# A new opening order with other fillers, branch hints, and a last store in two parts, in a fused three-layer kernel on one core

## The chip, the core and the metric

The kernel runs on one NeuronCore of a Trainium2 chip. The metric is device time in microseconds. Before the change three runs gave 753.0, 754.3 and 757.43 us, with a median of 754.3. The engines are called PE (TensorE; PEld is its weight load), DVE (VectorE), ACT (ScalarE), POOL (GpSimd) and SP (SyncE, which issues most transfers). A q behind a name (ACTq) marks an engine's sequencer, which runs branches, register loads, semaphore waits and transfer issues.

## The reference

Three layers follow one another on 4 batches of 768 rows and 384 columns, all in float32:

```python
# layer 1, gated linear attention, 4 batches x 8 heads x 768 rows x 48
f = 1.0 / (1.0 + np.exp(-f_logit))
for t in range(S):
    state = f[:, :, t, :, None] * state + einsum('bhd,bhe->bhde', k[:, :, t], v[:, :, t])
    y[:, :, t] = einsum('bhd,bhde->bhe', q[:, :, t], state)
# layer 2, x is y with the heads side by side
xn = (x - mean(x)) / sqrt(var(x) + 1e-06) * g_ln
x = x + maximum(xn @ w_ch1, 0) @ w_ch2             # 384 -> 1536 -> 384
# layer 3
h = maximum(x.T @ w_tok1, 0) @ w_tok2              # over the rows, 768 -> 256 -> 768
u = x + h.T
out = u + maximum(u @ w_ch1b, 0) @ w_ch2b          # 384 -> 1536 -> 384
```

## The kernel before

Layer 1 is cut into chunks of 128 rows: unit n is chunk n // 4 of batch n % 4, 24 units in all. The steps of a unit bear short names, and the prediction uses them. `n.lf`, `n.lq`, `n.lv` load the gate, q and k, and v. `log` and `cum` (L332) build running sums of the log gates with a matmul on a triangle of ones; `ek` and `eq` (L336, L340) take their exponentials on ACT; `km` and `qm` (L343, L346) scale k and q. `kp` (L355) transposes k on PE and `kt` (L246, L248) copies it out. `sc` (L378) forms the scores, `st` (L390) the new state, `A0` and `A1` (L400) mask the scores on DVE. `y` (L441) multiplies masked scores and v; `yw` (L456) is a small ACT operation, named `done` in the rows, that stands between `y` and `z`; `z` (L432) adds what the carried state contributes, in the same PSUM bank (tile `sc`). `stm`, `ste`, `std` carry the state on. `lna`, `lnc`, `lnv` are the layer norm, `tp`, `ah`, `al` the transposes into the MLP. `mS.*` are the pieces of an MLP group of layer 2, the first of its matmuls at L580 and L610.

The MLP weights arrive as 64-bit words and are turned into high and low float32r parts on chip; `wI.ld` is such a load and `wI.a`, `b`, `c`, `h`, `l` are the conversion steps. The big products are made of three matmuls of such parts (hh, lh, hl).

Each piece of work is a slot. Slots are emitted one after another and an engine executes its instructions in the order in which they were emitted, so the emitted order is the schedule of every engine at once, and the order of the transfers on SP too. For the opening, up to the end of unit 11's work, the order is the list `ORDER`, written out step by step; sets beside it choose the engine of a step (`POOL`, `OTHER`) or its PSUM bank (`AT`). Later slots are placed by a planner and stand as before.

A step written `n.step+k` gets fillers on PE ahead of it: matmuls on a tile of zeros that compute nothing. Ahead of `cum`, `kp`, `sc` and `tp` they are k matmuls of 224 columns (`busy`, L536 to L538) into the bank that the step is about to fill. Ahead of `y` they are 3k matmuls of 64 columns (L449) into a part of the `sc` tile. The first work of PE is `warm` (L734), 28 fillers of 224 columns.

The end: the last output chunk is added up on DVE (`fin`, L991), and its store is issued on ACT's queue (`put`, L995), while all earlier stores go through SP. Then each engine loads a flag (L1187) and branches on it (L1194): a general path for inputs outside the fast path's range lies behind that branch and is not taken here. The block after it (L1388) holds the waits for the transfers and the final barrier.

Of the kernel before, what the change touches and what calls it, by code (L numbers as in the profile page):

```python
# [51 lines left out]
ORDER = """
    0.lf 0.log 0.cum 1.lf 1.log 0.lq 0.ek 0.eq 1.cum+4 2.lf 0.lv 0.km 2.log 0.kp+4 0.qm 0.kt 1.eq 3.lf 1.ek 0.tot
    0.sc 1.lq w3.ld 1.tot 0.st 3.log 0.A1 0.A0 2.cum 0.stm 3.cum+9 1.qm 3.ek 0.y 3.tot 0.yw 1.km w3.a 0.z 2.ek
    2.eq 0.lna 1.sc+3 1.lv 2.lq w3.b 4.lf 1.kp w3.c 1.kt w5.ld 5.lf 1.st 0.ste 3.lq 0.lnc 1.A1 1.A0 2.km 1.stm
    0.tp+3 2.tot 3.eq 2.kp 1.y+3 4.log 2.qm 3.qm w5.a 0.lnv 1.yw 1.z 2.sc 0.ah 2.kt 4.cum 5.log 1.lna w5.b 0.al
    3.km 3.kp 2.lv 3.lv w3.h 4.lq 1.lnc 1.ste 2.st w5.c 2.A0 2.A1 1.tp 3.sc w3.l 0.std 4.ek w5.h 5.cum 1.ah w0.ld
    2.stm 2.y 4.eq 3.kt 5.eq 3.st 1.al 4.km 2.ste 3.A0 2.yw 2.z 4.qm 3.A1 3.y w0.a 6.lf 5.ek 4.kp 2.lna 7.lf 3.yw
    6.log 3.stm 2.lnc 4.lv w0.b 3.z w5.l 4.sc 7.log 5.tot 2.tp 4.kt w0.c 4.st w1.ld 6.cum w0.h 7.cum 3.ste 2.ah
    w1.a 3.lna 1.std 4.stm 4.A0 7.tot 4.A1 4.y 7.eq 6.tot 2.al 4.yw w1.b w4.ld 1.lnv 4.tot 5.lq w2.ld w1.c 5.qm  # L60
    m0.5 5.km w1.h w0.l 4.z w2.a 3.lnc 4.ste w16.ld m0.0 w1.l 5.lv 6.eq 6.ek 5.kp 7.ek 5.kt w4.a 5.sc 2.lnv 3.tp
    5.st w16.a w2.b w16.b w2.c m0.h0 w4.b m0.1 6.lq 5.A1 5.A0 m0.h5 3.ah w14.ld 5.stm m0.l5 m0.l0 w16.c 6.qm 4.lna
    5.y m0.3 6.km w13.ld 5.yw 5.z 4.lnc 3.al m0.h1 w2.h 3.lnv 6.kp 6.kt w2.l 5.lna 6.lv w17.ld w4.c 6.sc m0.2
    m0.l1 w14.a 4.tp w15.ld w16.h w14.b w4.h 5.lnc w4.l m0.h3 m0.l3 4.ah w14.c 4.al 6.st 5.tp 5.ah m0.4 m0.h4
    m0.h2 5.al w13.a w14.h 7.lq 7.km 6.A0 w13.b m1.5 w16.l 8.lv 9.lf m0.l2 w12.ld m1.2 m1.3 w12.a 6.A1 2.std m0.l4
    3.std m1.h2 m1.l2 w12.b 6.y 7.qm m1.h3 2.lnr w14.l w12.c 9.log w12.h m1.1 w15.a w7.ld 7.lv m1.h1 w13.c w12.l
    m1.4 5.ste w13.h m1.l3 m1.l1 6.yw 7.sc m1.h4 w15.b w13.l 7.kp w19.ld w11.ld w17.a m1.h5 7.kt w17.b w15.c w15.h
    4.std m1.0 w17.c w15.l m1.h0 m1.l4 m0.o20 7.st w17.h 6.stm m0.o10 w10.ld 8.lf m1.l0 w17.l 7.A0 w7.a m1.l5
    8.log w7.b w11.a w11.b 9.scan 6.z w10.a 9.tot 8.scan w7.c 8.eq 9.lv 6.ste w11.c 8.tot w7.h 7.A1 m1.o10 m0.o00
    8.ek w11.h m1.o11 8.lq m0.o11 m0.o01 8.qm w7.l 4.lnv 8.km w10.b 6.lna 7.y m0.r11 w8.ld 5.lnv m0.o21 m1.7 w19.a  # L70
    5.lnr m0.r01 w9.ld w10.c m0.r21 m1.r11 m1.o00 9.eq w10.h w19.b w10.l w11.l w6.ld w6.a m1.o20 w19.c 6.lnc w6.b
    w9.a 8.kp w9.b m1.o21 9.ek w6.c w19.h w19.l w8.a w8.b w6.h w9.c w20.ld m1.r21 s0.ld w22.ld 8.sc 7.yw 10.lf
    8.kt m1.o01 m1.r01 8.st m1.11 m1.h7 m1.h11 w9.h 8.A1 w6.l w22.a w22.b w8.c 7.stm 11.lf 7.ste w18.ld w21.ld
    10.log m1.6 m0.11 m0.h11 7.z w8.h m1.l11 m1.l7 w9.l m0.6 6.std 9.lq w18.a w18.b w8.l w20.a 9.km m1.h6 w18.c
    m0.7 8.A0 w18.h w20.b w23.ld m0.l11 m0.h6 11.log m0.9 w22.c w18.l w20.c m0.h7 m0.l7 m1.l6 7.lna w20.h m0.l6
    m0.h9 w21.a m1.8 m0.8 w21.b m0.l9 8.y 9.qm w20.l 9.kp 8.stm 7.lnc 10.scan w23.a m1.9 m0.h8 9.kt 8.yw m1.h8
    m1.l8 w23.b 10.ek m1.h9 w21.c m1.10 9.sc m0.l8 m1.h10 8.z w23.c 10.lq s1.ld 10.lv 9.st 8.lna s2.ld m1.l9 5.std
    w23.h 10.eq m0.10 w21.h w23.l 11.scan w21.l m0.o22 m0.h10 w22.h m0.l10 8.ste m1.o02 m1.l10 10.qm 9.A1 7.tp
    7.ah w22.l 6.tp m1.o03 7.lnv 9.A0 7.al 9.y 8.lnc 8.tp m1.r03 m0.o23 11.ek 6.lnv 11.eq 10.tot 10.km s0.a 7.std
    9.yw m1.o12 s1.a 8.lnv 6.ah 9.stm 8.std m0.r23 m1.d0 m0.d2 9.z s0.b 10.sc 10.kp 6.al 8.ah 8.al m0.o02 9.lna  # L80
    10.kt 9.ste m0.o12 9.std s0.c m1.o22 m0.o13 10.st 9.lnc 10.stm s1.b 11.lq m0.r13 m0.o03 s1.c 10.A1 m0.r03
    m1.o13 10.A0 10.ste m1.r13 m0.d1 m0.d0 m1.o23 10.std s3.ld 11.lv m1.d1 8.lnr s0.h
""".split()
# [23 lines left out]
class Slots:
# [1293 lines left out]
```

## Time and profile before

| | us |
|---|---|
| median of three runs | 754.3 (753.0 to 757.43) |
| the profiled execution: its own time | 753.65 |
| its span, first to last instruction | 751.9 |
| PE busy | 741.3 (99% of the span) |
| DVE, ACT, POOL busy | 502.4, 353.7, 119.6 |
| mean granted clock of PE | 0.996 of full speed |

The time of a run holds 1.75 us beyond the span (753.65 - 751.9). PE is busy nearly throughout. From 40 us to 740 us it hardly waits; what it does not use lies in the first 36 us and in the last 6 us.

### The profile page before, as it was taken

How to read it: one execution, taken by the hardware profiler on the slowest of the kernel's cores; microseconds unless marked ns; L12 is line 12 of the kernel's file. 1: busy time of each engine (PE TensorE's matmuls, PEld its weight loads, DVE VectorE, ACT ScalarE, POOL GpSimd, SP SyncE). 2: the span in 40 equal slices, each digit the busy share in tenths (PEclk: the TensorE clock that was granted, in tenths of full speed). 3: DMA queues.
4: the chain of work that ended last, by engine and by line, in shares of the span. 5: the costliest groups of instructions: out<-in, count | busy, mean ns of one | idle time of the engine just before them, and what ended most of it. 6: DMA issues, size and time to landing. Idle time of an engine off the chain costs nothing.

```text
span 751.9 us, 17197 instructions
## 1 busy us (share of the span) xinstructions
PE 741.3 (99%) x6981; PEld 723.5 (96%) x6981; DVE 502.4 (67%) x927; ACT 353.7 (47%) x890; POOL 119.6 (16%) x102
## 2 busy tenths in 40 slices
PE   8999999999999999999999999999999999999996
PEld 7889999999999999999999999999999999999996
DVE  3799886797787767674345655867468654868481
ACT  6756253544645446342223433745266442757340
POOL 2451212122244220200000100101000000102010
PEclk9999999999999999999999999999999999999999
DMA  9775422656576665743438748453433535344401
GB/s 254 225 258 163 148 96 91 216 181 211 160 264 195 186 188 158 218 150 117 128 101 291 268 168 308 144 169 134 135 90 105 176 106 152 95 146 119 119 16 69
DMA packets 62424, 122.52 MB, mean 163 GB/s; under 512 B 7040, under 2 KB 27904, under 8 KB 62336
## 3 DMA queue, kind: packets, MB, share of 16 engines
q1 hardware_dynamic: 62192, 121.14, 51.2%
q8 instruction: 57, 0.93, 0.5%
q14 instruction: 31, 0.25, 0.1%
q10 hardware_dynamic: 144, 0.20, 0.1%
HBM read 96.93 MB, written 24.38 MB: 161 GB/s over the span
## 4 chain that ended last, share of the span: by engine, by line
PE 93%; DVE 3%; ACT 2%; DMA 2%; issue 1%; SPq 0%; ACTq 0%
PE mo L610 20%; PE mo L987 19%; PE mm L580 18%; PE mm L934 18%; PE rt L854 3%; PE ht L876 3%; PE sc L441 2%; DMA cs<-in_w 2%; PE sc L432 2%; PE sc L378 1%; PE sc L390 1%; PE kp L355 1%; PE tp L544 1%; PE tp L888 1%; PE cum L332 1%; PE warm L734 1%
## 5 line engine op out<-in xcount | busy, mean ns | idle before, releaser
L580 PE MATMUL mm<-wx 128*128 128x384 f32 x864 | 159.1, 337 | 0.4 <-DVE hl L599 0.2
L580 PEld LDWEIGHTS mm<-wx 128*128 128x128 f32 x864 | 149.1, 188 | 1.3 <-DVE hl L599 0.8
L934 PE MATMUL mm<-xsh,wx 128*128 128x384 f32 x528 | 138.4, 335 | 0.3 <-DVE q L944 0.3
L610 PE MATMUL mo<-w2h,hh 128*128 128x384 f32 x288 | 98.7, 343 | 0.0
L987 PE MATMUL mo<-w2h,hh 128*128 128x384 f32 x288 | 97.2, 338 | 0.0
L934 PEld LDWEIGHTS mm<-xsh,wx 128*128 128x128 f32 x528 | 95.7, 188 | 1.2 <-DVE q L944 1.2
L610 PE MATMUL mo<-w2h,hl 128*128 128x384 f32 x288 | 96.4, 335 | 0.0
L610 PE MATMUL mo<-w2l,hh 128*128 128x384 f32 x288 | 96.3, 335 | 0.0
L987 PE MATMUL mo<-w2l,hh 128*128 128x384 f32 x288 | 96.3, 334 | 0.0
L987 PE MATMUL mo<-w2h,hl 128*128 128x384 f32 x288 | 96.3, 334 | 0.0
L934 PE MATMUL mm<-xsl,wx 128*128 128x384 f32 x264 | 88.3, 335 | 0.0
L974 POOL TENSOR_TENSOR hl<-u,hh 128x768 fp32r<-128x768 f32 x16 | 29.8, 1861 | 337.0 <-ACT u L969 244.3
L595 ACT ACTIVATE hh<-mm 128x384 fp32r<-128x384 f32 x96 | 46.2, 487 | 74.7 <-PE mm L580 71.3
L599 DVE SCALAR_TENSOR_TENSOR hl<-mm,hh 128x384 fp32r<-128x384 f32 x96 | 52.3, 551 | 20.5 <-ACT hh L595 20.0
L991 DVE TENSOR_TENSOR xr<-mo,xr 128x384 f32<-128x384 f32 x48 | 26.7, 555 | 53.2 <-PE mo L987 53.2
L1150 ACT ACTIVATE cs<-cs 128x384 f32<-128x384 f32 x56 | 31.1, 556 | 57.8 <-DVE cs L1147 57.6
L610 PEld LDWEIGHTS mo<-w2h,hh 128*128 128x128 f32 x288 | 54.1, 188 | 0.3
L987 PEld LDWEIGHTS mo<-w2h,hh 128*128 128x128 f32 x288 | 54.1, 188 | 0.1
L610 PEld LDWEIGHTS mo<-w2l,hh 128*128 128x128 f32 x288 | 54.2, 188 | 0.0
L987 PEld LDWEIGHTS mo<-w2l,hh 128*128 128x128 f32 x288 | 54.1, 188 | 0.0
L987 PEld LDWEIGHTS mo<-w2h,hl 128*128 128x128 f32 x288 | 54.1, 188 | 0.0
L610 PEld LDWEIGHTS mo<-w2h,hl 128*128 128x128 f32 x288 | 54.1, 188 | 0.0
(172 smaller groups left out, 1300.5 us busy)
## 6 DMA issues: line engine op xcount, KB each, us to landing
cs<-in_w SPq DMA_DIRECT2D x48, 384.0 KB, 3.2
sg<-in_w SPq DMA_DIRECT2D x44, 384.0 KB, 4.7
ts<-t_d SPq DMA_DIRECT2D x48, 256.0 KB, 2.9
wx<-f_d SPq DMA_DIRECT2D x12, 576.0 KB, 6.0
V<-in_v_n SPq DMA_DIRECT2D x21, 288.0 KB, 4.8
T<-in_k_t SPq DMA_DIRECT2D x21, 224.0 KB, 2.9
T<-in_q_t SPq DMA_DIRECT2D x21, 224.0 KB, 3.8
x_d<-x SPq DMA_DIRECT2D x24, 192.0 KB, 3.1
```

The source lines that it names most:

```text
L432: nc.tensor.matmul(t["sc"][half(i), r, D * p:D * p + D], t["Q"][rows(r), p, half(i)], s[rows(r), D * p:D * p + D], start=False, stop=p == ...
L580: nc.tensor.matmul(ps, w[:, f, k, :], x[:, k, :], start=(i == 0), stop=(i == 8))
L595: nc.scalar.activation(out=hid(f)[0], in_=t[f], func=AF.Relu)
L599: nc.vector.scalar_tensor_tensor(hl, t[f], 0.0, hh.bitcast(F32), op0=ALU.max, op1=ALU.subtract)
L610: nc.tensor.matmul(ps, x, w[:, f, :], start=(f == lo and i == 0), stop=(f == hi and i == 2))
L854: nc.tensor.matmul(t["r"][j], w, x, start=(s == 0 and i == 0), stop=(s == NCH - 1 and i == 2))
L876: nc.tensor.matmul(ps, w, x[:, j], start=(i == 0), stop=(i == 5))
L934: nc.tensor.matmul(ps, w, x, start=n == 0, stop=n == len(ops) - 1)
L974: le.tensor_tensor(l, whole(g, i), h.bitcast(F32), op=ALU.subtract)
L987: nc.tensor.matmul(ps, x, w[:, f], start=(g % 3 == 0 and m == 0 and n == 0), stop=(g % 3 == 2 and m == 1 and n == 2))
L991: nc.vector.tensor_tensor(us[b, u], t["o", u], us[b, u], op=ALU.add)
L1150: nc.scalar.activation(out=t["u"], in_=t["u"], func=AF.Abs, accum_out=wlow[:, i:i + 1])
```

## The change

It replaces `ORDER` and the sets beside it; it makes the fillers of `busy` 448 columns wide (two units in one matmul, an odd last one 224) and lets `warm` use them, with 25 units in place of 28; it stores the last output chunk as 256 and 128 columns, each by its own addition on DVE and its own issue on ACT, the second through the tile `ident`; and it emits a branch hint for SP, ACT and DVE near the end. The values of `LATER` are the same in another order.

```diff
- CHK=199, NV=12, WARM0=28, SG=5, PL=4, J=77)
+ CHK=199, NV=12, WARM0=25, SG=5, PL=4, J=77)
 ORDER = """
-    0.lf 0.log 0.cum 1.lf 1.log 0.lq 0.ek 0.eq 1.cum+4 2.lf 0.lv 0.km 2.log 0.kp+4 0.qm 0.kt 1.eq 3.lf 1.ek 0.tot
...
+    0.lf 0.log 1.lf 0.cum 0.ek 0.lq 0.km 2.lf 0.kp+17 0.lv 0.eq 1.log 1.cum+6 0.qm 0.kt 2.log 1.eq 1.ek 1.lq 0.sc
...
     def busy(ps, k):
-        for _ in range(k):
-            nc.tensor.matmul(ps[:, :224], zeros[:, 0], zeros[:, :, :112].to_broadcast([128, 2, 112]))
+        c = min(112, ps.shape[-1] // 4)
+        while k > 0:
+            n = 4 if k > 1 else 2
+            nc.tensor.matmul(ps[:, :c * n], zeros[:, 0], zeros[:, :, :c].to_broadcast([128, n, c]))
+            k -= 2
...
-        for _ in range(k):
-            nc.tensor.matmul(wt[0][:, :224], zeros[:, 0], zeros[:, :, :112].to_broadcast([128, 2, 112]))
+        busy(wt[0], k)
...
+        def fin(u, ch):
+            if ch and (b, u) == (B - 1, NCH - 1):
+                n = DM - 128
+                nc.vector.tensor_tensor(us[b, u][:, :n], t["o", u][:, :n], us[b, u][:, :n], op=ALU.add)
+                nc.scalar.dma_start(out=out[b, 128 * u:128 * u + 128, :n], in_=us[b, u][:, :n])
+                nc.vector.tensor_tensor(ident, t["o", u][:, n:], us[b, u][:, n:], op=ALU.add)
+            else:
+                nc.vector.tensor_tensor(us[b, u], t["o", u], us[b, u], op=ALU.add)
...
-            q = nc.scalar if (b, u) == (B - 1, NCH - 1) else nc.sync
+            if (b, u) == (B - 1, NCH - 1):
+                nc.scalar.dma_start(out=out[b, 128 * u:128 * u + 128, DM - 128:], in_=ident)
+            else:
+                nc.sync.dma_start(out=out[b, 128 * u:128 * u + 128, :], in_=us.pop((b, u)))
...
+    ahead = [mybir.EngineType.SP, mybir.EngineType.Activation, mybir.EngineType.DVE]
+    sl.e(end - 2, lambda: tc.mark_branch_hint_location("inside", "LikelyTaken", ahead))
...
-    with tc.If(flag < 1):
+    with tc.If(flag > 0, preferred_fallthrough_block=False, label="inside") as inside:
+        pass
+    with inside.Else():
```

Fillers behind `warm`, in the order in which PE meets them, were `1.cum+4`, `0.kp+4`, `3.cum+9`, `1.sc+3`, `0.tp+3`, `1.y+3`: 23 of 224 columns and 9 of 64. They are now `0.kp+17`, `1.cum+6`, `0.y+10`, `2.kp+3`, `1.y+13`, `3.y+3`, `5.sc+13`: 39 units of 224 columns and 78 matmuls of 64. `8.km` moves from DVE to POOL.

The first place is PE behind the state of unit 0. Before, its last two matmuls (L390) are followed by the running sum of unit 2 and the nine fillers ahead of unit 3's.

```order
L390 MATMUL sc<-firstv,kt 64x48
L390 MATMUL sc<-firstv,kt 48x48
L332 MATMUL cum<-tri,first 112x128 x4
L538 LDWEIGHTS zeros
L538 MATMUL cum<-zeros 128x224
L538 LDWEIGHTS zeros
```

Now the fillers of `0.y` stand there (line 449 as before), 30 pairs of which the first begin here.

```order
L390 MATMUL sc<-firstv,kt 64x48
L390 MATMUL sc<-firstv,kt 48x48
L449 LDWEIGHTS zeros
L449 MATMUL sc<-zeros 128x64
L449 LDWEIGHTS zeros
```

Behind the `y` of unit 0 (L441) PE now runs the following; L332 is a running sum, of unit 2 and then of unit 3.

```order
L441 MATMUL sc<-W,A 64x48 x2
L332 MATMUL cum<-tri,first 112x128 x4
L432 MATMUL sc<-mid,first 64x48 x8
L355 MATMUL kp<-ident,first 128x112 x4
L332 MATMUL cum<-tri,F 112x128 x4
L378 MATMUL sc<-first 64x64 x16
```

So both running sums have moved from ahead of `0.y` to behind it, one ahead of `0.z` and one between `1.kp` and `1.sc`.

The second place is the end of ACT's program. Before, the last two activations of the MLP (`hh`) are followed by the store, the load of the flag (`oki`) and the branch.

```order
L966 ACTIVATE hh<-q 128x768
L966 ACTIVATE hh<-u 128x768
L995 DMA out<-xr 128x384
L1187 TENSOR_LOAD oki
L1194 COMPARE_AND_BRANCH
```

Now a hint and a second store stand there.

```order
L968 ACTIVATE hh<-q 128x768
L968 ACTIVATE hh<-u 128x768
L1402 BRANCH_PREFETCH_HINT
L996 DMA out<-xr 128x256
L1003 DMA out<-ident 128x128
L1199 TENSOR_LOAD oki
L1206 COMPARE_AND_BRANCH
```

The hint follows the last activation, ahead of both stores. On SP it stands between the fourth and the fifth of the last stores, and on PE and POOL there is none.

The third place is the end of DVE's program, where the six additions of `fin` stood in one row ahead of the flag's load. Now it reads as follows.

```order
L999 TENSOR_TENSOR xr<-mo,xr 128x384 x4
L1402 BRANCH_PREFETCH_HINT
L999 TENSOR_TENSOR xr<-mo,xr 128x384
L995 TENSOR_TENSOR xr<-mo,xr 128x256
L997 TENSOR_TENSOR ident<-mo,xr 128x128
L1199 TENSOR_LOAD oki
L1206 COMPARE_AND_BRANCH
```

The sixth addition has become two, of 256 and 128 columns, and the hint stands ahead of the fifth.

## Rows read from the trace of the kernel before

**Rows 1.** Waits of PE, first 40 us: line, what ended it, total us, times, longest

```profile
PE sc L378 <- issue: 0.9, 1, 0.9
PE sc L390 <- DVE kt L246: 0.7, 1, 0.7
PE sc L432 <- ACT done L456: 0.6, 2, 0.3
PE sc L432 <- ACT ek L336: 0.3, 1, 0.3
```

**Rows 2.** Windows: busy us of each engine, PEclk granted clock, DMA share, GB/s

```profile
15.00:20.00 5.00, 3.40 (x78) 2.82 (x77) 2.46 (x7) 2.51 (x10) 2.53 (x2) 0.91 1.07 282
19.20:22.60 3.40, 3.08 (x51) 2.79 (x51) 2.13 (x6) 1.04 (x4) 0.78 (x1) 0.51 1.07 272
```

**Rows 3.** Chain that ended last, opening, fillers and their neighbours: start, us, what

```profile
1.05 4.99 PE warm L734 x28
...
6.92 0.38 PE cum L538 x4
...
8.18 0.38 PE kp L538 x4
...
10.39 1.06 PE cum L332 x8
11.45 0.86 PE cum L538 x9
12.31 0.89 PE cum L332 x8
...
14.79 0.40 PE sc L538 x3
...
18.88 0.41 PE tp L538 x3
...
20.68 0.48 PE sc L449 x9
```

**Rows 4.** Timeline of DVE, 9 to 14 us, the masks of unit 0

```profile
10.53 0.76 DVE L400 TENSOR_TENSOR A<-sc,upper 128x256 f32<-128x256 f32 x2 [0.87 <-PE sc L390]
```

**Rows 5.** Groups by shape to 160 us: count, busy us, mean ns, idle before

```profile
L343 POOL TENSOR_TENSOR T<-T,ek 112x512 f32<-112x512 f32 x5 | 7.9, 1575 | 14.9 <-DMA T<-in_k_t 13.1 <-ACT ek L336 1.8
L343 DVE TENSOR_TENSOR T<-T,ek 112x512 f32<-112x512 f32 x5 | 3.4, 681 | 0.0
```

**Rows 6.** Waits of PE, 100 to 742 us

```profile
PE mm L934 <- DVE q L944: 0.3, 1, 0.3
```

**Rows 7.** Timeline, the end: last matmul, last addition, last store

```profile
745.32 0.34 PE L987 MATMUL mo<-w2h,hl 128*128 128x384 f32 x1
745.70 0.56 DVE L991 TENSOR_TENSOR xr<-mo,xr 128x384 f32<-128x384 f32 x1 [2.57 <-PE mo L987]
746.29 0.38 ACTq L995 DMA_DIRECT2D out<-xr  x1
```

**Rows 8.** Tile out, 735 to 752 us: the four last stores together

```profile
DMA to landing us min/median/max: 1.9/2.6/4.3
```

**Rows 9.** Instructions of L1194, the branch and the first waits behind it

```profile
L1194 DVEq COMPARE_BRANCH  x1: 72/72/72, 746.3 to 746.3; - x1
...
L1194 ACTq COMPARE_BRANCH  x1: 54/54/54, 747.2 to 747.2; - x1
L1194 DVEq EVENT_SEMAPHORE  x1: 21/21/21, 749.5 to 749.5; - x1
L1194 ACTq EVENT_SEMAPHORE  x1: 17/17/17, 750.3 to 750.3; - x1
```

**Rows 10.** Instructions of L1388 on SP, the waits and the barrier at the end

```profile
L1388 SPq EVENT_SEMAPHORE  x10: 17/28/28, 750.6 to 751.9; - x10
```

**Rows 11.** Transfers, 745.5 to 752 us, by queue: packets, MB, share

```profile
q14 instruction: 5, 0.04, 2.6%
q8 instruction: 1, 0.02, 1.0%
```

More of the change, by code (lines that the diff above doesn't have):

```diff
@@ L46 @@
 P = dict(A=[7, 10, 16, 22, 30, 38, 46, 54, 62], M0=29, LEAD=7, WS=9, WD=2.2, CS=0.5, JQ=42, JD=3.8, JL=6, CKS=16, CKD=3.2, CKL=3.2,
-         CHK=199, NV=12, WARM0=28, SG=5, PL=4, J=77)
+         CHK=199, NV=12, WARM0=25, SG=5, PL=4, J=77)
 POOL = set("""
-    1.km 2.km 2.qm 3.qm w3.l 0.std 4.qm w5.l 1.std w0.l w1.l 6.km w2.l w4.l 7.km w16.l 2.std w14.l w12.l 4.std
-    w15.l w10.l w6.l w8.l 9.km 9.qm w22.l 11.km 11.qm 11.std
+    1.qm 1.std 3.km 0.std w1.l 4.km w3.l 5.km w5.l 6.km 3.std w12.l 7.qm w13.l w14.l 8.km w7.l 4.std w8.l w6.l
@@ L51 @@
+    9.km w19.l 5.std w18.l w23.l w21.l 11.km 11.qm 11.std
 """.split())
 ORDER = """
-    0.lf 0.log 0.cum 1.lf 1.log 0.lq 0.ek 0.eq 1.cum+4 2.lf 0.lv 0.km 2.log 0.kp+4 0.qm 0.kt 1.eq 3.lf 1.ek 0.tot
-    0.sc 1.lq w3.ld 1.tot 0.st 3.log 0.A1 0.A0 2.cum 0.stm 3.cum+9 1.qm 3.ek 0.y 3.tot 0.yw 1.km w3.a 0.z 2.ek
-    2.eq 0.lna 1.sc+3 1.lv 2.lq w3.b 4.lf 1.kp w3.c 1.kt w5.ld 5.lf 1.st 0.ste 3.lq 0.lnc 1.A1 1.A0 2.km 1.stm
-    0.tp+3 2.tot 3.eq 2.kp 1.y+3 4.log 2.qm 3.qm w5.a 0.lnv 1.yw 1.z 2.sc 0.ah 2.kt 4.cum 5.log 1.lna w5.b 0.al
@@ L57 @@
[L57 to L76, printed above, removed]
@@ L82 @@
-    m1.o13 10.A0 10.ste m1.r13 m0.d1 m0.d0 m1.o23 10.std s3.ld 11.lv m1.d1 8.lnr s0.h
+    0.lf 0.log 1.lf 0.cum 0.ek 0.lq 0.km 2.lf 0.kp+17 0.lv 0.eq 1.log 1.cum+6 0.qm 0.kt 2.log 1.eq 1.ek 1.lq 0.sc
+    0.st 0.A0 0.A1 0.y+10 3.lf 0.tot 0.yw 3.log w3.ld 1.km 0.stm w3.a 2.cum w3.b 0.z 1.kp 2.ek w3.c 0.lna 1.lv
+    3.cum 2.lq 1.tot 4.lf 1.kt w3.h 2.eq 1.qm 0.ste 0.lnc 1.sc 1.st 0.tp 3.ek 3.eq 1.stm 2.tot 2.km 2.kp+3 4.log
+    2.qm 2.kt 1.A0 2.lv 6.lf 1.ste w1.ld 1.std 2.sc 2.st 1.A1 2.A1 3.tot w1.a w2.ld 4.cum w1.b 6.log 2.A0 3.lq
@@ new lines @@
+    5.lf w2.a 3.km 1.y+13 4.ek 1.yw 4.eq 0.ah 2.y 3.lv 4.tot w2.b 1.z w1.c 2.stm 1.lna 0.std 2.yw 2.z 0.al 4.lq
+    w1.h 3.qm 1.lnc 0.lnv w1.l w0.ld 3.kp 4.km 2.lna w2.c 3.kt 6.cum 2.lnc 7.lf 3.sc 1.tp 5.log 1.ah 3.st w4.ld
+    2.ste 3.A0 2.tp 3.stm 3.A1 1.lnv w3.l 5.cum 2.ah 3.ste 3.y+3 6.tot 2.al 1.al 2.lnv 3.yw w0.a 5.eq 5.ek 4.qm
+    4.kp 3.z w0.b w2.h w0.c m0.3 3.lna 5.tot 4.sc w2.l w4.a 4.kt m0.h3 6.ek 4.lv 6.eq 3.lnc w5.ld m0.1 w4.b 4.st
+    5.lq w5.a w4.c w5.b 7.log 4.A1 3.tp 3.ah 4.A0 m0.2 w13.ld w0.h 4.stm w4.h m0.h1 5.km 3.al 4.y 4.yw 5.qm 4.ste
@@ new lines @@
+    5.kp w5.c 5.sc+13 5.kt 4.z 5.lv w12.ld w0.l m0.l3 3.lnv m0.h2 5.st 6.lq w5.h w14.ld m0.l1 w15.ld 7.cum 5.stm
+    w5.l 6.km w4.l 4.lna 5.A0 5.A1 m0.0 4.lnc w12.a m0.l2 7.eq 5.y 7.tot m0.h0 w13.a 2.std 5.yw 7.ek 4.tp 5.z
+    m0.l0 m0.4 5.lna 6.kp 5.lnc 5.tp 4.ah 7.lq 4.lnv 5.ah 6.kt m0.5 4.al 6.qm w13.b w17.ld 8.lf 5.al m0.h5 m0.h4
+    w12.b 6.lv w12.c w14.a 7.km 3.std m1.2 m0.l4 m1.3 w12.h w12.l w16.ld 5.ste 8.log w13.c m0.l5 10.lf m1.h3 w7.ld
+    w14.b w15.a 7.lv 6.sc m1.1 8.scan m1.h1 m1.l3 6.st m1.4 m1.l1 7.kp w14.c w13.h 7.qm 6.A0 6.stm m1.0 m1.h4 7.kt
@@ new lines @@
+    w13.l w14.h m1.h2 m1.h0 6.A1 5.lnv w17.a 8.tot 7.sc 6.y m1.l2 w14.l w10.ld m1.5 6.yw m1.l0 6.ste m1.l4 w15.b
+    w15.c w16.a w15.h 6.z m1.h5 2.lnr m1.o20 8.lv 6.lna w17.b m0.o00 7.st m1.o00 w17.c 10.lv w16.b w16.c w17.h
+    8.eq w9.ld w17.l w22.ld 5.lnr w16.h m1.l5 w16.l w10.a 7.A1 w15.l w8.ld m0.o10 w9.a 10.log w10.b w10.c w10.h
+    8.lq w7.a w9.b m1.o01 8.ek 8.km w10.l 8.qm w6.ld 7.A0 m0.o01 m1.r01 w7.b w9.c w8.a 7.y w7.c m1.o10 m1.o21
+    m0.r01 8.kp m1.o11 w7.h m1.r21 9.lf w7.l 6.lnc 9.log w6.a w8.b m1.r11 m0.10 w9.h w9.l 4.std m0.o20 10.scan
@@ new lines @@
+    w20.ld w6.b w8.c w6.c 7.stm w20.a m0.o11 w21.ld w18.ld w8.h m0.o21 m0.r11 w20.b w6.h w8.l m0.h10 m0.9 8.kt
+    m0.8 w6.l 7.ste m0.r21 9.lv w20.c w18.a m1.9 8.sc m0.l10 7.yw m0.h9 w20.h m0.h8 w11.ld w11.a w19.ld 9.scan
+    w11.b m0.l8 m1.h9 w20.l w19.a 7.z 9.lq 8.st m0.l9 10.eq 10.ek m1.7 w19.b w19.c w11.c s0.ld w11.h 9.eq 8.A1
+    7.lna w18.b w11.l w23.ld 9.ek m1.h7 m1.l7 w22.a m1.l9 m1.6 m1.8 8.A0 w19.h m1.h8 w18.c 8.stm m1.11 m1.h11
+    m1.l11 m0.6 w22.b m1.h6 m0.11 9.km m1.l8 m1.l6 7.lnc 9.qm 8.y w19.l 8.yw m0.h11 9.tot 9.kp m0.7 m0.h7 w18.h
@@ new lines @@
+    w23.a 5.std 11.lf m0.l11 w22.c w23.b 8.z w18.l s1.ld 9.sc m0.l7 8.ste 6.tp m0.h6 m1.10 m0.l6 6.ah 9.kt 9.st
+    w21.a 7.tp m1.h10 w23.c w21.b w21.c w23.h m1.l10 w21.h 7.ah m0.o12 w23.l 6.al 9.A1 11.log w22.h 6.lnv 9.stm
+    10.lq m0.o22 m1.o12 w22.l 10.km 9.A0 10.tot 7.al 8.lna w21.l s1.a 9.y m0.o13 8.lnc 10.qm 11.scan 9.yw 8.std
+    8.tp m0.r13 m1.o13 m0.o23 9.z m0.d1 m1.o02 m0.r23 9.ste 7.lnv 10.sc 10.kp m1.o03 m1.r13 10.kt s1.b 8.lnv 11.eq
+    9.lna 10.st m0.o02 s0.a s0.b m1.o22 8.lnr s0.c s0.h s3.ld 9.lnc 6.std 10.stm 10.ste 8.ah 7.std m0.o03 10.std
@@ L83 @@
+    m1.r03 10.A0 8.al m0.d2 10.A1 s1.c m0.r03 11.ek m1.d1 9.std s2.ld 11.lv 11.lq m1.o23 m0.d0 m1.d0
 """.split()
-LATER = dict(log=-12.25, tp=11.55, kt=-6.25, qm=-6.5, lq=-12.75, lnc=7.5)
+LATER = dict(lnc=7.5, tp=11.55, log=-12.25, qm=-6.5, lq=-12.75, kt=-6.25)
 VECTOR = set("""
@@ L97 @@
 AT = set("""
-    cum0 kp1 cum4 m0.0 kp6 tp4 m1.5 o000 o100 m0.11 m0.9 m1.9 o101 o111
+    cum0 cum3 cum6 m0.2 m0.4 m1.1 m1.0 o000 kp8 m0.8 m1.6 m0.7 m1.10 o021 kp10 o121
 """.split())
 OTHER = set("""
-    0.kt 0.stm 1.kt 2.kt 2.stm 3.kt 4.kt w16.h w14.h w19.h w6.h w8.h 10.kt
+    0.kt 1.kt w3.h 1.stm 2.kt w1.h 3.kt 8.kt w11.h w23.h w22.h 10.kt
 """.split())
@@ L988, in mm2 @@
                                          stop=(g % 3 == 2 and m == 1 and n == 2))
-        def fin(u):
-            nc.vector.tensor_tensor(us[b, u], t["o", u], us[b, u], op=ALU.add)
+        def fin(u, ch):
[6 more added lines that the diff above has]
+                nc.vector.tensor_tensor(us[b, u], t["o", u], us[b, u], op=ALU.add)
         def put(u):
-            q = nc.scalar if (b, u) == (B - 1, NCH - 1) else nc.sync
-            q.dma_start(out=out[b, 128 * u:128 * u + 128, :], in_=us.pop((b, u)))
+            if (b, u) == (B - 1, NCH - 1):
+                nc.scalar.dma_start(out=out[b, 128 * u:128 * u + 128, DM - 128:], in_=ident)
+            else:
+                nc.sync.dma_start(out=out[b, 128 * u:128 * u + 128, :], in_=us.pop((b, u)))
         return dict(prod=prod, copy1=copy1, add2=add2, add3=add3, add4=add4, hi=hi, rel=rel, lo=lo, mm2=mm2, fin=fin, put=put)
@@ L1068, in O @@
             if gs[-1] % 3 == 2:
-                sl.e(e + QS, lambda: Z["fin"](u))
+                sl.e(e + QS, lambda: Z["fin"](u, ch))
                 if ch:
```

5 lines of the change are left out of this document (removed).

## The prediction

> **What bounds the kernel now.** The page comes first: PE is busy for 741.3 of 751.9 us, so a change can gain only in the roughly 10 us in which PE doesn't work, by work of PE that is left out, or behind PE's last matmul. The waits of PE say where the 10 us lie. In the first 40 us PE waits four times in the middle of its work, 2.5 us together: 0.9 with no engine named ("issue"), 0.7 for a copy on DVE, 0.6 in two parts for the small ACT operation between `y` and `z`, and 0.3 for an exponential on ACT [rows 1]. From 100 to 742 us the largest wait is 0.3 us [rows 6]: there PE alone sets the pace. [...] The chain shows what fillers cost: they are matmuls like others in PE's row, so one that covers no wait lengthens the opening by its whole duration [rows 3]. At the end, the last matmul stops at 745.66 (745.32 + 0.34) and the last store is issued at 746.29 [rows 7]. The four last stores landed 1.9 to 4.3 us after their issue, and the last one was the slowest [rows 8]: 746.29 + 4.3 = 750.6, which is when SP's last waits begin; they and the barrier end at 751.9 [rows 10]. So 6.2 us pass behind the last matmul.
>
> I make the sum against the profiled execution (753.65 us) and apply the difference to the median, 754.3, which lies 0.65 above it.
>
> **The opening: what PE has to do.** *Warm.* 28 fillers took 4.99 us, 178 ns each [rows 3]. Three fewer units are worth -0.53 us. In the longer form a unit might cost a little less; I count nothing for it.
>
> *Fillers of 224 columns.* Five groups of 4, 4, 9, 3 and 3 took 0.38, 0.38, 0.86, 0.40 and 0.41 us, 2.43 in all [rows 3]. At the 95 ns of the first three groups 39 units take 3.7 us: +1.3. By the mean of all five (106 ns) it would be +1.7.
>
> *Fillers of 64 columns.* Nine took 0.48 us [rows 3], in the stretch where the clock was 0.51, so 53 ns each and about 27 at full clock. The 78 of the change take 2.1 us at full clock and 4.2 at half: +1.6 to +3.7, and I take +1.6. These stand ahead of `y` in PE's order, but they write the same tile and go behind the masks that `y` waits for, so I expect them to cover no wait for the masks; what they can do is keep PE busy.
>
> Together -0.5 + 1.3 + 1.6 = +2.4 us of PE's time, if none of it lies in a wait.
>
> **The opening: waits.** Of the 17 units ahead of `0.kp`, nothing is new: before, `1.cum` and eight units stood between `0.cum` and `0.kp`; eight units are 0.76 us and a running sum 0.89 to 1.06 [rows 3], together 1.7 to 1.8, and 17 units are 1.6.
>
> A new wait I can price is that of the masks of unit 0. `A0` and `A1` start when the last `st` matmul is done and take 0.76 us for both [rows 4]. Before, 1.06 + 0.86 + 0.89 = 2.81 us of PE work lay between `st` and `y` and covered that [rows 3]; now only fillers that wait with `y` stand there. With the 0.14 us between 10.39 and 10.53 and as much again on the way back PE stands for about 1.0 us. Queued behind are the two running sums, and so the exponentials of units 2 and 3. But those two sums, 1.95 us of real work, now stand behind `0.y`, one ahead of `0.z` and one ahead of `1.sc`, and can cover one of the two 0.3 us waits for ACT and the 0.7 us wait for the copy [rows 1]. The 0.9 us wait on nothing I leave as it is, since what causes it is not named. Balance: +1.0 - 0.3 - 0.7 = 0. The bounds are far apart. If the fillers' real purpose is met and all waits go, it is -2.5 us [rows 1]; if the moved sums make later units late and every wait stays beside the new one, with the next unit's masks bare in the same way, it is +2.0. I take 0, the row for the masks being the only one that measures the new place.
>
> *The clock.* Half speed over 3.08 us of busy time costs half of it, 1.5 us [rows 2]. What PE did before: 3.40 of 5 us busy, in a window in which the clock then fell. The change has more fillers behind that place (`2.kp+3`, `1.y+13`, `3.y+3`) and moves the waits to earlier places, so I take it that the low stretch doesn't come back: -1.5. The bounds are -1.5 and 0, or +1.5 if a second such stretch comes behind the wait at `0.y`.
>
> *`8.km` on POOL* takes 1.58 us in place of 0.68 [rows 5], so unit 8's transposes may come 0.9 us later. PE's other work stands ahead of them and no wait there is over 0.3 us [rows 6], so 0, with 0.9 as the upper bound. The other moves of steps between engines, banks and the order of loads have no row of their own and go into the bounds of the waits.
>
> Opening: +2.4 + 0 - 1.5 = +0.9 us, bounds -1.6 (all waits gone) and +5.
>
> **The end.** Before: matmul done 745.66, addition 745.70 to 746.26, issue 746.29. The change adds 256 columns first. Two masks of 256 columns took 0.76 us, so about 0.4 each [rows 4]; the addition of 384 took 0.56 [rows 7], which makes about 0.3 for 128. DVE ends at about 746.1 and 746.4. ACT needs 0.38 us for an issue [rows 7], so the second issue starts at about 746.5, 0.2 later than the only one did before. What follows depends on the landing, for which no row shows a 128-column store. By the fastest of the four last stores it lands at 748.4, by the median of 2.6 at 749.1, by the slowest at 750.8 [rows 8]. SP's waits and the barrier took 1.3 us from there [rows 10]; the last part is on a counter that SP waits for first, so the waits for the other counters, which had been over before it landed, now follow. Ten waits fit in that 1.3 us, so seven more are under 0.9; 17 to 28 ns each [rows 10] make 0.1 to 0.2; I take 0.5. Ends: 750.2, 750.9 or 752.6, against 751.9: -1.7, -1.0 or +0.7. I take -1.0, the median, because there is a reason for the slow one: after 745.5 us instruction transfers ran beside the last store [rows 11], and ACT and DVE each stood for 3.0 to 3.2 us between their branch and their next instruction (747.2 to 750.3, 746.3 to 749.5) [rows 9]. If the hints bring these fetches forward, they leave the way of the store. PE has no hint, and its fetch remains.
>
> [...]
>
> Sum: +0.9 - 1.0 = -0.1 us, so **754.2 us**: no change that a measurement of this kernel can tell, for which I take 0.5%, or 3.8 us, as the bound. Its own range is 752.5 to 756.
>
> **Rivals.** *Slower: the fillers are work and the clock falls all the same.* The bare wait at `0.y` (+1.0), and a low stretch behind it or at the next units, put the clock term at 0 and leave the kt wait in place (+0.7): +2.4 + 0.7 + 0 = +3.1, and -1.0 at the end: 756.4. A second low stretch (+1.5) makes it 757.9, and with the 0.9 of `8.km` it passes 0.5%. For it: PE idle for 1.6 of 5 us went with a low clock [rows 2], and fillers behind a wait don't fill it. Against: two sums now cover waits that stood bare. Chance 0.23, of which 0.08 beyond 758.1.
>
> *Faster: the fillers stand where PE waited.* All 2.5 us of waits go, so the added 2.4 us are paid for, and the clock stays up: -1.6, with the end at its fast bound -1.7: 751.0. Beyond 0.5% it goes only if several waits that I don't see in the rows (later steps made earlier) give something too. Chance 0.19, of which 0.10 beyond.
>
> *The hints do nothing, or PE's own fetch holds the last store.* ACT then branches later, by the 0.4 us of the second issue, stands for 3.1 us more [rows 9], and goes on at about 750.7, where SP's last waits begin now; the store lands by its slowest, 752.6: +0.9 + 0.7 = +1.6, so 755.9. For it: the gaps [rows 9]; the last store was the slowest of four [rows 8]. Against: the hint stands ahead of both stores on ACT and ahead of the fifth addition on DVE, so there is time before the branch for a fetch. Chance 0.18. [...]
>
> **Numbers.** The forecast has 0.40; the three rivals 0.23, 0.19, 0.18. The range that leaves out two in ten reaches from 751.0, the faster rival, to 757.0, above the third rival and most of the first. Faster by over 0.5%: 0.10. Slower by over 0.5%: 0.09. Within: 0.81.
>
> **What would show it.** In the profile after: fillers of 64 columns at about 27 ns in the chain, 2 us of them; a wait of about 1 us ahead of `0.y` with DVE's masks as its cause; a granted clock of 1.00 between 15 and 25 us, or, if I am wrong, near 0.5 in a stretch there; the first matmul of L580 about 1 us later than before. At the end: two issues on ACT 0.4 us apart, landings near 2.6 us, and gaps behind ACT's and DVE's branches much under 3 us if the hints work. The forecast is wrong if the waits between 6 and 36 us add up to over 4 us or under 1, or if the time between PE's last matmul and the end, 6.2 us before, comes out under 4 or over 7.

## The result: 0.6% slower, and the profile after

The changed kernel takes 759.46 us (median of 9 runs, 755.65 to 763.35) against 755.44 us of before (9 runs). The ratio is 1.0063, with an interval of 1.0041 to 1.0086. The prediction was 754.2 us, and its range ended at 757.0: it was wrong, on the slow side. "Slower by over 0.5%" had a chance of 0.09.

The profiled execution took 758.5 us with a span of 756.8 us, 4.9 more than before. The page's first table, in the same columns as the table of before:

```profile
PE 742.8 (98%) x7033; PEld 722.4 (95%) x7033; DVE 505.7 (67%) x930; ACT 353.6 (47%) x889; POOL 117.3 (16%) x101
```

The waits of PE in the first 40 us, beside [rows 1]:

```profile
PE sc L432 <- DVE mid L246: 1.5, 1, 1.5
PE warm L540 <- DVE zeros L646: 1.1, 1, 1.1
PE sc L449 <- DVE A L400: 0.9, 1, 0.9
PE cum L332 <- issue: 0.6, 1, 0.6
```

And the same view from 40 to 745 us; in the kernel before it has nothing over 0.3 us there ([rows 6] show it from 100 us on):

```profile
PE kp L355 <- POOL T L343: 2.8, 1, 2.8
PE mm L583 <- DVE hl L602: 0.2, 1, 0.2
PE mm L936 <- DVE q L946: 0.2, 1, 0.2
```

The reader is to see that the opening's waits changed their places more than their sum (2.5 us before, 3.1 after, the wait for `zeros` left aside), and that a new wait of 2.8 us stands far behind the places that the prediction looked at. The windows, with the columns of [rows 2]:

```profile
15.00:20.00 5.00, 5.00 (x115) 4.27 (x116) 4.07 (x9) 4.59 (x16) 0.00 (x0) 1.00 0.50 139
19.20:22.60 3.40, 2.68 (x76) 2.20 (x74) 2.09 (x6) 2.32 (x7) 0.51 (x1) 1.00 1.00 322
```

The stretch at the lower clock is gone: 1.00 in place of 0.51. The chain that ended last shows where the 2.8 us come from (start, us, what):

```profile
130.55 0.32 SPq L675
...
132.92 0.50 SPq L312
...
133.52 6.31 DMA T<-in_k_t
...
139.99 1.28 POOL T L343
...
141.31 0.60 PE kp L355 x4
```

The row of waits names POOL, but POOL had itself been waiting for a load: the k of unit 11 (`11.lq`) was issued at 133.52 us and took 6.31 us to land. In the new `ORDER` the step stands near the very end of the list, behind the stores of the converted weights on SP; in the old one it stood 18 steps before the end, and SP's row in the kernel before reads:

```profile
120.52 0.33 SPq L300 DMA_DIRECT2D T<-in_k_t  x1
```

The fillers, in the chain's rows as in [rows 3]:

```profile
7.11 1.61 PE kp L540 x9
...
9.19 0.57 PE cum L540 x3
...
12.66 1.03 PE sc L449 x30
...
32.80 0.42 PE sc L449 x9
```

```profile
42.93 1.23 PE sc L540 x7
```

The nine `kp` rows are the 17 units ahead of `0.kp`, and the last row is the 13 units ahead of `5.sc`. The nine fillers at 32.80 are those of `3.y`; the 39 of `1.y` don't stand on the chain. The end, with the views of [rows 7] and [rows 9]:

```profile
750.16 0.34 PE L989 MATMUL mo<-w2h,hl 128*128 128x384 f32 x1
...
750.53 0.42 DVE L995 TENSOR_TENSOR xr<-mo,xr 128x256 f32<-128x256 f32 x1 [2.57 <-PE mo L989]
750.87 0.28 DVE L997 TENSOR_TENSOR ident<-mo,xr 128x128 f32<-128x128 f32 x1
750.99 0.39 ACTq L996 DMA_DIRECT2D out<-xr  x1
751.41 0.45 ACTq L1003 DMA_DIRECT2D out<-ident  x1
```

```profile
L1206 SPq EVENT_SEMAPHORE  x8: 17/17/17, 754.9 to 755.4; - x8
...
L1206 PEldq COMPARE_BRANCH  x1: 3625/3625/3625, 747.8 to 747.8; - x1
...
L1206 DVEq COMPARE_BRANCH  x1: 84/84/84, 751.2 to 751.2; - x1
...
L1206 ACTq COMPARE_BRANCH  x1: 68/68/68, 752.5 to 752.5; - x1
L1206 DVEq EVENT_SEMAPHORE  x1: 21/21/21, 754.4 to 754.4; - x1
L1206 ACTq EVENT_SEMAPHORE  x1: 17/17/17, 755.3 to 755.3; - x1
```

The first part landed 1.9 us after its issue, the second 3.4 us (751.4 to 754.9). From the last matmul (750.50) to the end it is 6.3 us, 6.24 before: the new end gave nothing in this execution. So the 4.9 us were lost before PE's last matmul, which stops at 750.50 in place of 745.66.

### The profile page after: what moved, and what is told of

The parts are those of the page before. It is cut to its first block, busy times and chain, and to the rows that moved or that the text cites. A ratio compares the mean times of both kernels' runs of the same rounds, so it can differ in the third digit from the quotient of the medians.

```text
span 756.8 us, 17305 instructions
## 1 busy us (share of the span) xinstructions
PE 742.8 (98%) x7033; PEld 722.4 (95%) x7033; DVE 505.7 (67%) x930; ACT 353.6 (47%) x889; POOL 117.3 (16%) x101
## 4 chain that ended last, share of the span: by engine, by line
PE 90%; DVE 4%; DMA 2%; ACT 2%; issue 1%; SPq 0%; POOL 0%; DVEq 0%; POOLq 0%; ACTq 0%
PE mo L989 20%; PE mo L613 19%; PE mm L583 18%; PE mm L936 16%; PE ht L878 3%; PE rt L856 3%; PE sc L441 2%; PE sc L432 1%; PE sc L378 1%; PE tp L547 1%; PE sc L390 1%; PE kp L355 1%; PE tp L890 1%; DMA cs<-in_w 1%; DMA T<-in_k_t 1%; DMA firstv<-in_w 1%
```

## The experiments

The theory after the result: 2.8 of the 4.9 us are the late load of unit 11, which needs neither the fillers nor the engines to be explained; the fillers cost about what they save in clock; the end is worth nothing. Rivals: POOL makes the wait, the rest of the order makes it, the fillers are pure loss, or the end is at fault. All ratios are to the kernel before, run beside them.

**The load moved back** (e1), in the changed kernel:

```diff
-    8.tp m0.r13 m1.o13 m0.o23 9.z m0.d1 m1.o02 m0.r23 9.ste 7.lnv 10.sc 10.kp m1.o03 m1.r13 10.kt s1.b 8.lnv 11.eq
+    8.tp m0.r13 m1.o13 m0.o23 9.z m0.d1 m1.o02 m0.r23 9.ste 7.lnv 10.sc 10.kp 11.lq m1.o03 m1.r13 10.kt s1.b 8.lnv 11.eq
-    m1.r03 10.A0 8.al m0.d2 10.A1 s1.c m0.r03 11.ek m1.d1 9.std s2.ld 11.lv 11.lq m1.o23 m0.d0 m1.d0
+    m1.r03 10.A0 8.al m0.d2 10.A1 s1.c m0.r03 11.ek m1.d1 9.std s2.ld 11.lv m1.o23 m0.d0 m1.d0
```

> The changed kernel with one step moved: the loads of k and q of unit 11 stand earlier in the order, ahead of the stores of the converted weights on SP, in place of near the end of the list. Theory: the 2.76 us wait of PE at 138.6 us, in front of unit 11's transposes, comes from the load of k, which was issued at 133.52 and landed 6.31 us later; with it early PE waits under 0.5 us there and the kernel takes 2.3 to 2.8 us less than the changed kernel, a ratio to before of about 1.003. Rival: the wait is the multiplication on POOL (1.28 us) or work queued ahead of it there, as the row names POOL as the releaser; then at least 1.3 us of the wait stay. Second rival: PE loses elsewhere what it gains here, ratio 1.006 as measured for the change.

Measured: 755.39 us against 755.13, ratio 1.0017 (1.0001 to 1.0033). The load of k was issued at 123.2 us, and from 100 to 200 us PE has one wait left:

```profile
PE mm L583 <- DVE hl L602: 0.2, 1, 0.2
```

The wait is gone although `11.km` is still on POOL, and the ratio fell by 0.46%, 3.5 us, of which 2.76 are the wait seen (the rest is within the intervals; e3 below shows what else the late load can cost). The opening's waits stayed (1.6, 0.9 and 0.6 us). The rival of POOL falls, and so does the one that PE loses elsewhere what it gains here.

**The same load moved late in the kernel before** (e5):

```diff
-    10.kt 9.ste m0.o12 9.std s0.c m1.o22 m0.o13 10.st 9.lnc 10.stm s1.b 11.lq m0.r13 m0.o03 s1.c 10.A1 m0.r03
+    10.kt 9.ste m0.o12 9.std s0.c m1.o22 m0.o13 10.st 9.lnc 10.stm s1.b m0.r13 m0.o03 s1.c 10.A1 m0.r03
-    m1.o13 10.A0 10.ste m1.r13 m0.d1 m0.d0 m1.o23 10.std s3.ld 11.lv m1.d1 8.lnr s0.h
+    m1.o13 10.A0 10.ste m1.r13 m0.d1 m0.d0 m1.o23 10.std s3.ld 11.lv 11.lq m1.d1 8.lnr s0.h
```

> The kernel before with one step moved: the loads of k and q of unit 11 stand at the end of the order, behind the load of v of unit 11, as in the change. Theory: they are issued at about 132 us in place of 120.5, land 3 to 6 us later, and with 1.3 us on POOL PE waits 2 to 5 us ahead of unit 11's transposes; the kernel takes 2 to 5 us more, a ratio of 1.003 to 1.007. Rival: the wait needs the rest of the new order too (POOL and SP busier there); then no wait and a ratio within 0.2% of 1.

Measured: 757.65 us against 754.31, ratio 1.0053 (1.0033 to 1.0072). The load of k was issued at 133.52 us, as in the change, and landed 4.8 us later. The waits of PE have the same row as in the changed kernel, with nothing else of the change in it:

```profile
PE kp L355 <- POOL T L343: 2.8, 1, 2.8
```

So the step alone makes the wait, in either order.

**The old end in the changed kernel** (e2): the lines of `fin` and `put`, the hint and the `If` as before.

> The changed kernel with the end of before: one addition and one store for the last chunk, no hints. Theory: the new end is worth nothing (6.24 us from the last matmul to the end before, 6.30 after), so the ratio to before stays at 1.005 to 1.008 and the end stays at 6.0 to 6.5 us. [...] Other rival: the new end costs, and this kernel is 0.5 us or more faster.

Measured: 759.54 us, ratio 1.0062 (1.0041 to 1.0083), the same as the change. The end took 5.5 us here (last matmul 754.16, span 759.7). PE's wait for unit 11 was 3.7 us in this profile. The end isn't what made the kernel slower.

**The new end in the kernel before** (e4): the diff of the end alone.

> The kernel before with the new end alone: the last store in two parts, and the hints. Theory: no change that can be measured, ratio 0.998 to 1.001, the time from the last matmul to the end 5.9 to 6.5 us, and the gaps behind the branches of ACT and DVE stay at 2.8 to 3.2 us. Rival, from the prediction: with the fetch out of the way the last part lands by the median of 2.6 us, and the end is 1 us shorter, ratio 0.9987.

Measured: 755.21 us against 755.13, ratio 1.0009 (0.9988 to 1.003); from the last matmul to the end 6.45 us (746.05 to 752.5). The two parts landed after 3.9 and 3.7 us. No gain.

**The hints alone** (e11), the store in one part, in the kernel before:

> The kernel before with the hints alone and the last store in one part. Theory: nothing changes, the gap behind ACT's branch 2.8 to 3.2 us, the end 5.2 to 6.3 us as in the kernels with the old end, ratio 0.9985 to 1.0015. Rival: the hints help and the second store and its waits eat it; then the end is 1 us or more under 5.2.

Measured: 753.89 us against 754.6, ratio 0.9988 (0.9966 to 1.001). The end took 5.6 us, and between the branch and the next instruction ACT stood for 2.9 us (748.5 to 751.4) and DVE for 3.0 (747.5 to 750.5). The hints on these engines do nothing that these rows show.

**A hint on PE too** (e10), with the new end, in the kernel before:

```diff
-    ahead = [mybir.EngineType.SP, mybir.EngineType.Activation, mybir.EngineType.DVE]
+    ahead = [mybir.EngineType.PE, mybir.EngineType.SP, mybir.EngineType.Activation, mybir.EngineType.DVE]
```

> The kernel before with the new end and a hint on PE too. Theory: hints bring no fetch forward on any engine (the gaps behind ACT's and DVE's branches were 2.8 and 3.2 us with a hint, 3.1 and 3.2 without), so PE's instruction transfer still runs beside the last store and the end stays at 6.0 to 6.9 us, ratio 0.999 to 1.003. Rival: PE's own fetch is what holds the last store, and a hint on PE moves it: landings of both parts near 1.9 us and an end of 4.5 to 5.2 us, ratio 0.998 to 0.9995.

Measured: 753.24 us against 754.6, ratio 0.9982 (0.9958 to 1.0006), which no interval tells from 1. The rows of the branch do tell (the view of [rows 9]):

```profile
L1204 SPq EVENT_SEMAPHORE  x8: 17/17/17, 748.9 to 749.4; - x8
L1204 PEldq COMPARE_BRANCH  x1: 495/495/495, 742.9 to 742.9; - x1
...
L1204 PEldq EVENT_SEMAPHORE  x1: 51/51/51, 745.6 to 745.6; - x1
...
L1204 ACTq COMPARE_BRANCH  x1: 68/68/68, 747.5 to 747.5; - x1
...
L1204 ACTq EVENT_SEMAPHORE  x1: 17/17/17, 750.2 to 750.2; - x1
```

PE's branch takes 0.5 us in place of 3.6, and PE goes on 2.7 us after the branch began (3.6 before). The second part of the store landed after 2.4 us, and the end took 5.5 us (745.54 to 751.0), between what the theory and what the rival expected. In the six kernels with the new end and no hint on PE the second part landed after 2.7 to 4.0 us. In the closing block SP's row is

```profile
L1400 SPq EVENT_SEMAPHORE  x10: 17/28/290, 749.5 to 751.0; - x10
```

Its longest entry, 290 ns (28 in the change), is a wait for ACT, which goes on only at 750.2, when SP's waits for the stores had been over since 749.4. With the store early, the gap behind ACT's branch ends last, and a still earlier landing would have gained nothing here.

**No fillers ahead of y** (e3), in the changed kernel:

```diff
-    ... 0.y+10 ... 1.y+13 ... 3.y+3 ...
+    ... 0.y ... 1.y ... 3.y ...
```

> The changed kernel without the 78 fillers of 64 columns ahead of y of units 0, 1 and 3. Theory: they cover no wait, so leaving them out gives back 2 to 2.7 us of PE's time, ratio to before about 1.003, if the clock holds. Rival: they keep the clock up; without them a stretch of about 3.4 us at half speed comes back between 12 and 30 us, worth 1.5 us, and waits grow by a part of what is left out, so that the gain is under 1 us.

Measured: 762.48 us, ratio 1.0111 (1.0082 to 1.0141), against 1.0063 for the change, though PE has 78 matmuls less. The mean granted clock of its six runs lay between 0.988 and 0.995; the nine of the change lay between 0.993 and 0.999. Two windows of its profile:

```profile
26.00:29.00 3.00, 3.00 (x23) 2.68 (x18) 2.94 (x6) 2.09 (x8) 1.80 (x2) 0.50 0.51 180
142.00:145.40 3.40, 3.40 (x13) 3.40 (x12) 0.00 (x0) 0.79 (x2) 0.76 (x1) 0.51 0.00 0
```

The first stretch at the lower clock lies behind the place of the missing fillers. The second does not: it begins where PE's wait for unit 11 ends, 3.5 us here, for the late load is still in this kernel. The profile of e2, with all fillers and the late load, has such a stretch at the same place, from the end of a wait of 3.7 us on:

```profile
143.80:146.90 3.10, 2.83 (x11) 2.83 (x12) 0.00 (x0) 0.54 (x1) 1.45 (x2) 0.50 0.03 11
```

The profiles of the change and of e5, where the wait was 2.76 us, have none. So in some executions the late load costs half of PE's time in such a stretch on top of the wait, 1.4 us in e2 and 1.7 in e3, and e3 mixes this loss with that of the fillers. The theory of this expectation, that the fillers are pure loss, falls; how much of the loss is theirs, e3 doesn't show. The next runs have the early load. Which of the three groups does it:

**Only those of unit 1 left out** (e6), with the early load:

```diff
-    5.lf w2.a 3.km 1.y+13 4.ek ...
+    5.lf w2.a 3.km 1.y 4.ek ...
```

> The changed kernel with the early load of unit 11 and without the 39 fillers of 64 columns ahead of y of unit 1. Theory: it is these that hold the clock between 23 and 30 us; without them a stretch at the lower clock appears after 23 us, and the 1.0 to 1.3 us that they take are lost again by it: 0 to 2 us slower than the early load alone (ratio to before 1.002 to 1.004). Rival: the fillers only take PE's time, and the kernel is 1.0 to 1.3 us faster than with them (ratio 1.000 to 1.0005).

Measured: 757.09 us, ratio 1.0031 (1.0014 to 1.0049), against 1.0017 with them; the intervals overlap, so the time alone doesn't settle it. The profiled execution, the slowest of twelve (760.42), shows two rows of the price, a wait of PE in the middle of unit 1's `y` and a window:

```profile
24.09 0.26 PE L441 MATMUL sc<-firstv,A 64*64 64x48 f32 x2 [0.93 <-DVE A L400]
28.00:37.00 9.00, 9.00 (x117) 8.02 (x115) 6.02 (x15) 4.15 (x13) 3.57 (x3) 0.50 0.54 179
```

The wait of 0.93 us is for the second half of unit 1's masks, which DVE reached late because a weight load (`firstv<-in_w`) had kept it idle for 0.97 us (1.49 us ahead of the same masks in the changed kernel). The change and e1 don't have it: there the fillers stand where PE would wait, so of the 1.1 us that they take some 0.2 is extra. Then come nine us at the lower clock, with PE busy throughout. In eight of the twelve runs the mean clock was at 0.995 or under; with the fillers (e1) this was so in two of twelve. So the clock is lost more often without them, though not in each execution.

**Only those of unit 0 left out** (e7), with the early load:

```diff
-    0.st 0.A0 0.A1 0.y+10 3.lf ...
+    0.st 0.A0 0.A1 0.y 3.lf ...
```

> The changed kernel with the early load of unit 11 and without the 30 fillers of 64 columns ahead of y of unit 0. Theory: those of unit 1 hold the clock, so this one keeps it, and about half of the 1.0 us that these fillers take comes back: ratio 1.000 to 1.0015. Rival: the missing work of PE at 12 us, behind the bare 0.95 us wait, brings a stretch at the lower clock between 14 and 25 us, and the kernel is 0.5 to 1.5 us slower than with the early load alone (ratio 1.0025 to 1.004).

Measured: 755.2 us against 754.31, ratio 1.0004 (0.9987 to 1.0021). The clock held (0.999 in the profile, 0.995 to 0.999 in the runs) and by the ratios the 1.0 us came back, again with intervals that overlap. The wait for the masks is the same with and without them, 0.95 us: those of unit 0 stand behind it and cover nothing. The nine ahead of `3.y` were left out only in e3, and no run shows what they do.

**Long fillers and a shorter warm-up in the kernel before** (e8): the diff of `busy`, `warm` and `WARM0` alone.

> The kernel before with the fillers of 448 columns and 25 units of warm-up in place of 28, the order as before. Theory: worth almost nothing, -0.5 to 0.5 us, ratio 0.999 to 1.001; the wait on nothing that the rows show moves from 16 us to a later place, since PE's program has some 50 instructions less ahead of it. Rival: fewer units of warm-up leave the clock low longer (the first running sum took 1.21 us after the shorter warm-up in the changed kernel and 0.88 before), and the kernel is slower by 0.5 us or more.

Measured: 753.59 us against 754.31, ratio 0.9994 (0.9979 to 1.001). Its waits in the opening are a warning against single executions:

```profile
PE sc L390 <- issue: 2.3, 1, 2.3
PE kp L355 <- issue: 2.1, 1, 2.1
```

These two waits on nothing that the profile names are 4.4 us, in place of 0.9 before, and yet the granted clock was 1.00 in every window of 5 us from 5 to 40 us. In ten of its twelve runs the mean clock was at 0.997 or above, in the kernel before in 14 of 33: the longer fillers seem to keep the clock up in the old order too, yet the time shows no gain.

**Fewer fillers, early load, old end** (e9): e7 without the 13 units ahead of `5.sc`, and with the end of before.

> The changed kernel with the early load of unit 11, without the fillers of y of unit 0 and without the 13 units ahead of sc of unit 5 (1.40 us of PE at 41 us, where PE has no wait beside them), and with the end of before. Theory: the 1.4 us come back, and 0.5 at the end: ratio to before 0.998 to 0.9995, the first version here that is not slower than before. Rival: these fillers too hold the clock or stand in a wait; then the ratio stays at 1.000 to 1.001, as without them removed.

Measured: 753.33 us against 754.6, ratio 0.9985 (0.9961 to 1.001), as the theory had it, but with an interval that holds the rival's 1.000 too. **The same with the new end and a hint on PE** (e12):

> The changed kernel with the early load of unit 11, without the fillers ahead of y of unit 0 and sc of unit 5, with the store in two parts and hints on SP, ACT, DVE and PE. Theory: the order is worth the 0.15% that it gave with the old end, and PE's hint shortens the end to 5.0 to 5.5 us where it was 5.4 with the old end in that order: ratio to before 0.996 to 0.9985. PE's branch takes about 0.5 us in place of 3.6. Rival: the shorter end seen with the hint on PE was one execution's luck; then the end is 6 us or more and the ratio 0.998 to 1.0.

Measured: 753.72 us against 753.36, ratio 0.9994 (0.9979 to 1.0009). PE's branch took 0.49 us, the second part landed after 2.4 us and the end took 5.4 us (746.60 to 752.0), as in e10. The time is the rival's, the end the theory's: the shorter end came in both kernels with the hint, one profiled execution of each, but it is no shorter than the old end in this order (5.4 us in e9, 744.56 to 750.0). No version here beats the kernel before by more than its interval.

## Why the prediction was wrong, point by point

*The step that failed* is the last sentence on `8.km`: "The other moves of steps between engines, banks and the order of loads have no row of their own and go into the bounds of the waits", together with the choice of 0 for everything behind 40 us because "no wait there is over 0.3 us". The order of the loads did have rows: the landing times, and the place of each load on SP. A wait that is absent before says only that the load was early enough before. The load of unit 11 went from 120.5 us (where e5 took it from) to 133.5, and its 2.76 us of wait, with the lower clock that can follow it (e2, e3), were in no term and in no rival. With the load early (e1) the ratio is 1.0017, 756.7 us on the scale of the result's 755.44, inside the range.

*Fillers of 224 columns.* 39 units took 3.69 us, as predicted: 1.61, 0.57 and 1.23 us on the chain, and about 0.28 for the three of `2.kp`, which stand only in the timeline. They read 0.45 there; I take off 0.17, by which the group of `5.sc` reads longer in the timeline (1.40) than on the chain. *Of 64 columns:* 30 took 1.03 us, 34 ns each, not 27, and all 78 took 2.58 in place of 2.1 (1.03 and 0.42 on the chain, and 1.30 - 0.17 for the 39 of unit 1, by the same correction). Against the 2.91 of before that is +3.36 for both where I had +2.9: the term was mis-sized. That all 78 cover no wait for the masks holds for unit 0 only; those of unit 1 stand in one of 0.93 us (e6).

*Warm.* 4.85 us in place of 4.99: -0.14, not -0.53. The longer form has no price that these rows show: the same 25 units took 4.22 (e12) to 4.85 us, and the 28 of before 4.24 (e11) to 5.04 (e5). One profiled execution doesn't size this term, and why it varies is open.

*The masks.* Right: a wait of 0.95 us ahead of the fillers of `0.y`, named as DVE's masks, and the two running sums behind it covered the wait for the copy and one for ACT. But a wait of 1.53 us for a copy on DVE came in front of `z` (27.4 us), which I had not priced. On the chain that copy comes behind DVE's work on a weight load that landed late:

```profile
17.82 5.46 DMA firstv<-in_w
...
26.99 0.28 DVE mid L246
```

This again is the place of a load in the order, though no run moved this one. The opening's waits went from 2.56 to 3.11, +0.55 where I took 0.

*The clock.* The lower stretch of the opening is gone, as forecast. Of the eight profiles with the new order the six with the fillers of `1.y` show 1.00 in every window of 5 us from 5 to 50 us, and the two without them (e3, e6) a lower stretch behind 26 us; so one of the two reasons given, more fillers, is borne out, and e8 says that their length may do it as well. The size was not quite right: the 3.08 us of the term hold the 0.48 us of fillers that another term had taken out already, so 0.24 of the 1.5 was counted twice. And the late load brought a lower clock back at 142 us in some executions: over its nine runs the change's median clock is 0.996, the same as that of the kernel before.

*`8.km` on POOL.* Right, 0: no wait there.

*The end.* Wrong: +0.06 in place of -1.0. The issue times were about as worked out (0.49 us from matmul to first issue, 0.42 between the two). The first part lands after 1.9 us, but the second after 3.4: the third rival, PE's own fetch beside the last store, is what e10 and e12 speak for, since with a hint on PE that landing is 2.4. It is not shown, for each is one profiled execution, and e1 had 2.7 without that hint. Also, the 6.24 us of before were the longest of the six profiles with the old store (5.2 to 5.6 in the other five), while the new end without a hint on PE took 5.7 to 6.9. So in the profiles the new end is rather longer than the old one, by an amount that the times don't show (e2, e4). ACT and DVE stood about as long with a hint as without: 2.8 and 3.2 us between branch and next instruction, 3.1 and 3.2 before. PE's branch took 0.5 us with a hint (e10, e12) and 3.6 before.

Sum by what was measured: -0.14 (warm) + 3.36 (fillers) - 1.5 (clock) + 0.55 (waits of the opening) + 2.76 (load) + 0.06 (end) = 5.1, against 4.9 in the span. The last three terms are sound: together they are 3.4 us, by which PE's unused time grew (10.6 to 14.0). PE's own terms are rougher than the match looks: the clock is counted 0.24 too high, and the first running sum, 1.21 us in place of 0.88, is in none.

*The signs.* Neither sign of being wrong came: the opening's waits were 3.1 us (bounds 1 and 4) and the end 6.3 (bounds 4 and 7). Both look at places that were not at fault. The first matmul of L580 came at 34.97 us in place of 36.00, earlier and not 1 us later, with other work ahead of it.

What stays open: what PE waits for in the "issue" rows, which were 0.4 to 2.3 us each and moved from kernel to kernel. The 14 profiles have 19 of them of 0.5 us or more between 6 and 40 us, and each ended 1.9 to 3.1 us behind an instruction packet of 0.02 MB on queue q8 (2.7 us in the kernel before, 2.4 in the changed one). That speaks for late instruction transfers, but five of the six such packets between 6 and 40 us in the kernel before had no such wait behind them, nor had four of the five in the changed one, and no run tests it. Open, too, is why the lower stretch lasts 3.4 us in one execution and 9 in another, and how often the late load brings one.

## What to carry to other kernels

When a change rewrites an order, go through the loads first: for each, its new place on the issuing queue, its issue to landing time there, and who needs it; a wait that the old trace doesn't have can be made by moving one line (2.8 us in e5), and a long wait can be paid for twice, once as a wait and once by the clock behind it (3.7 and 1.4 us in e2). A filler is judged by a run without it: the wait that the fillers of unit 1 stood in (0.93 us, e6) shows only when they are gone, and the clock then fell to 0.50 behind it, while the 30 of unit 0 could go without harm that the intervals show. Where a list has several edits, undo each alone: here one step out of several hundred held over half of the loss.
